# Weights of q and k loaded ahead of the last scratch reads, and projections in the first cycle with scores

## The chip, the cores and the metric

The kernel runs on one core of one Trainium2 chip. A core has TensorE (PE, matmuls), VectorE (DVE), ScalarE (ACT), GpSimd (POOL) and SyncE (SP, which here issues most of the DMAs), a local memory, and eight accumulator banks that TensorE writes and VectorE and ScalarE read. The metric is the device time of one execution in microseconds.

## The reference, cut to what matters

A layer norm of x feeds two branches whose sum is added to x: attention with 32 heads of 16, and a gated MLP whose gate mixes along the sequence.

```python
S, D, H, Dh, Fh = 2048, 512, 32, 16, 896
xn = layernorm(x)
q, k, v = split(xn @ wqkv)                       # per head: S x 16
o = softmax(q @ k.T * Dh ** -0.5) @ v
A = o @ wo
z = gelu(xn @ w_in)
z1, z2 = z[:, :Fh], layernorm(z[:, Fh:])
g = w_sp @ z2 + b_sp[:, None]
out = x + A + (z1 * g) @ w_out
```

## The kernel before, in words

**Number format.** Each dense operand is split into a high and a low part. A dense product is three matmuls (mm3, lines 170 to 172): high by high, low by high, high by low. The split of a weight is a copy (line 196, GpSimd) and a subtraction (line 197, GpSimd).

**Attention.** Heads go in 16 pairs. For each pair there are two passes over the 2048 x 2048 products of q and k. The first finds each row's maximum: `max_mm` (line 650, result "mx") and a reduction on VectorE (line 658, "mm"). The second makes the scores (line 960, "st") from q and k with two more rows that hold the negated maximum, ScalarE takes the exponential (line 58, "pf"), and a matmul with V follows (line 934, "o"). A pair has 64 steps for maxima and 64 for scores. The maxima run LEAD = 27 steps ahead of the scores. When the 16 maxima of a quarter are there, they go through a small scratch (`mscr`) back into rows of q by four SP transfers.

**Where q and k come from.** The projections of q and k come in four blocks of 128 columns, m = 0 to 3, each for four quarters g of the sequence. The block m = 0 is made in the start, before the loop. The blocks 1 to 3 are made by the generator `qk_rest` inside the loop: `qk_group(m, g, ...)` makes a group of 12 matmuls for q (a = 0) and one for k (a = 1). ScalarE copies a group's bank ("qr"), copies its high part ("qkhl"), GpSimd subtracts (line 325), and SP stores the pair to scratch (`qscr`, `kscr`). There are three such buffers. `load_stacks(p)` reads a pair's rows from the scratch into one of two stacks, `qst` and `kst`, with eight transfers; in the start it does so for each quarter.

**The start.** x is loaded, normed, transposed (line 276) and split. Then come, for g = 0 to 3, the groups of m = 0, `load_stacks(0)` for that quarter, and four tiles of V (`v_tile`). The weights of m = 1 are begun (a load) at g = 2 and ended (the split) at g = 3. The weights of m = 2 and 3 are left to `qk_prepare()`, which is put on the list `bg` after the start. `bg` is moved on by one turn per half-step: a turn may start one load (three buffers "raw"), and may split a load that is two half-steps old.

**The loop.** It goes by half-steps, `now[0]` from -18. An even half-step has one maximum and two scores, an odd one two maxima and one score; two half-steps make a cycle of three steps. The 18 half-steps below 0 are called the lead in this document: they have maxima but no scores. In a half-step the dense work is taken from `queue` as long as a credit lasts. In the lead the credit is 2600 per half-step, that is four mm3 of 650, one group. From half-step 0 on, dense work goes only into odd half-steps, at a credit that spreads the work left over the steps left. A generator that lacks its weights returns a pause, and the half-step stays without dense work. All orders are written out in Python when the program is made. On the chip each engine, and each DMA queue, runs its own list in order and waits for semaphores.

**Banks.** Six of the eight banks are three double tiles that maxima and scores take in turn. The last two are called "d" (dense results) and "o" (the product with V). In the start the tiles of V take "d" and "o" in turn. In the lead a group takes "d" for q and "o" for k until half-step -3, and "d" from then on, since "o" belongs to the product with V from the first score cycle on.

Of the kernel before, what the change touches and what calls it, by code (L numbers as in the profile page):

```python
# [23 lines left out]
NG = S // 512  # L24
# [16 lines left out]
def fused_block(ctx, tc, x, wqkv, wo, w_in, w_spT, b_sp, w_out, out):  # L41
# [65 lines left out]
    now = [-2 * LEAD // 3 - 1]  # L107
# [3 lines left out]
    pool = [-1000.0]  # L111
# [41 lines left out]
    def dpsum(nm, tag="d", n=1):  # L153
        left[0] = n
        return ps.tile([P, 512], F32, tag=tag, name=nm, bufs=1)
# [13 lines left out]
    def mm3(acc, lh, ll, rh, rl, first, last):  # L169
        nc.tensor.matmul(acc, lh, rh, start=first, stop=False)  # L170
        nc.tensor.matmul(acc, ll, rh, start=False, stop=False)  # L171
        nc.tensor.matmul(acc, lh, rl, start=False, stop=last)  # L172
# [53 lines left out]
    bg = []  # L226
# [73 lines left out]

    def qk_group(m, g, w, tags=("d",)):
        for a in range(2):
            if now[0] < -2 and m:
                tags = ("d", "o")
            acc = dpsum(f"qk{m}_{a}_{g}", tags[a % len(tags)], ND)
            for c in range(ND):
                t = xnT[g, c]
                mm3(acc, w[a][:, 0, c * P:(c + 1) * P], w[a][:, 1, c * P:(c + 1) * P], t[:, 0, :], t[:, 1, :], c == 0, c == ND - 1)
                yield 650 + 0.5 * (c == ND - 1)
            if m == 0:  # L310
                run(qk_split(m, g, a, acc))
                yield 0
                continue
            raw_ = t512(f"qr{m}_{a}_{g}")
            act(raw_, acc, AF.Copy, 512)
            side.append(qk_split(m, g, a, raw_))
            yield 0

    def qk_split(m, g, a, src):
        hl = hilo(f"qkhl{m}_{a}_{g}")  # L320

        act(hl[:, a, :], src, AF.Copy, 512)
        yield
        if m:
            gps(1.3).tensor_sub(hl[:, 1 - a, :], src, hl[:, a, :].bitcast(F32))  # L325
            yield from pool_done()
        else:
            dve(512).tensor_sub(hl[:, 1 - a, :], src, hl[:, a, :].bitcast(F32))
        (store if m else move)((qscr, kscr)[a][m][:, :, g * 512:(g + 1) * 512], hl)
        yield  # L330

    def qk_prepare():
        yield from prepare(wq, [((m, a), *qk_weights(m, a)) for m in (2, 3) for a in range(2)])
# [15 lines left out]
    def v_tile(t, ws, mid=None):  # L349
        acc = dpsum(f"v{t}", "do"[t % 2])  # L350
        sl = slice((t % 4) * P, (t % 4 + 1) * P)
        for c in range(ND):
            if c == 2 and mid:
                mid(t + 1)
            xt = xnT[t // 4, c]
            mm3(acc, xt[:, 0, sl], xt[:, 1, sl], ws[c][:, 0, :], ws[c][:, 1, :], c == 0, c == ND - 1)
        act(vhead[:, t, :, :DH], acc.rearrange("p (h d) -> p h d", d=DH), AF.Copy, 512)
# [257 lines left out]
    def load_stacks(p, cols=slice(0, S)):  # L615
        m, r = p // 4, (p % 4) * 2
        q, k = qst[p % 2], kst[p % 2]
        sl = [slice((r + j) * DH, (r + j + 1) * DH) for j in range(2)]
        for j in range(2):
            for i, (t, scr) in enumerate(((q, qscr), (k, kscr))):  # L620
                two = t[64 * j:64 * j + 2 * DH, cols], scr[m][sl[j], :, cols]
                one = t[64 * j + 2 * DH:64 * j + KS, cols], scr[m][sl[j], i, cols]
                for args in (two, one):
                    if p and 2 * j + i:
                        later(2 * j + i, move, *args)
                    else:
                        move(*args)
# [200 lines left out]
    def run(gen):  # L828
        for _ in gen:
            pass  # L830
# [9 lines left out]
    with tc.manual_schedule(engines=engines):  # L840
# [46 lines left out]
        for g in range(NG):  # L887
            once = True
            for y in qk_group(0, g, w0, ("d", "o")):
                if y == 0 and once and g < 2:  # L890
                    once = False
                    if g == 0:
                        turn_x(1)
                        norm = norm_x(2)
                    else:
                        next(norm)
            load_stacks(0, slice(g * 512, (g + 1) * 512))
            if g == NG - 2:
                for a in range(2):
                    wq[1, a] = begin(*qk_weights(1, a))  # L900
            if g == NG - 1:
                for a in range(2):
                    wq[1, a] = end(wq[1, a])
            for t in range(4 * g, 4 * g + 4) if g else ():
                next(norm, 0)
                if t % 4 == 2:
                    if g + 1 < NG:
                        turn_x(g + 1)
                    if g + 2 < NG:
                        norm = norm_x(g + 2)  # L910
                v_tile(t, wv)
        steady.append(True)
        bg.append(qk_prepare())
        queue.extend([qk_rest(), z2_all(), z1_all(), spatial(), mlp_out(), attn_out()])
        todo = 650 * (3 * 32 + 112 + 112 + 28 * 16 + 112)
        pause = 0
# [78 lines left out]
        for half in range(-2 * LEAD // 3, 2 * (N // 3 + 4)):  # L995
            b = 3 * (half // 2)
            ms = [b + LEAD] if half % 2 == 0 else [b + LEAD + 1, b + LEAD + 2]
            ns = [n for n in ([b, b + 1] if half % 2 == 0 else [b + 2]) if 0 <= n < N]
            if b + LEAD >= NSTEP:
                ns = [n for n in range(b, b + 3) if n < N] if half % 2 == 0 else []  # L1000
            now[0] = half
            flush()
            for n in ns:
                if n == 16:
                    init_rows(1)
                if n % 64 == 14 and n // 64 + 1 < NP:
                    load_stacks(n // 64 + 1)
            pause = max(0, pause - 1.5)
            final = []
            if NSTEP - LEAD <= b < N and half % 2 and turn and turn[0][0] + 1 in added:  # L1010
                final.append(last_mm(*turn.pop(0)))
            tiles = [(scores, n) for n in ns]
            for i, m in enumerate(ms):
                tiles.insert(1 if half % 2 == 0 else 2 * i, (max_mm, m))
            for make, n in tiles:
                make(n)
            while ended:
                chunk_out(*ended.pop(0))
            for n in ns[:1]:
                exp(n)  # L1020
            if half % 2 == 0:
                pv_some(b - 1, ready // 2 * 2)
            for n in ns[1:]:
                exp(n)
            while behind and behind[0][0] <= half:
                nc.scalar.dma_start(*behind.pop(0)[1:])
            for f in final:
                last_add(*f)
            low = min(load.values())
            for e in load:  # L1030
                load[e] = min(load[e] - low, 2.0)
            limit = load["D"] + (2.5 if half % 2 == 0 else 3.0)
            for m in ms:
                max_red(m)

            if half % 2 == 0:
                for m in range(ms[0] - 2, ms[0] + 1):
                    max_fin(m)
            if drain:
                drain = False  # L1040
                cost = next(queue[0], None)
                if cost is None:
                    queue.pop(0)
                else:
                    pause = -cost
            bg[:] = [g for g in bg if next(g, 0) is None]
            side[:] = [g for g in side if load["D"] > limit or next(g, 0) is None]
            ready += len(ns)
            if b < 0:
                credit = 2600  # L1050
            elif half % 2:
                credit = min(credit + 3 * (max(todo / max(DENSE - b, 10), 600 if b > DENSE - 15 else 0) if todo > 0 else max((todo + 64 * 650) / max(N - 6 - b, 8), 450)), 3250)
            else:
                continue
            if urgent and between and not drain and "ones" in sel:
                queue.insert(0, urgent.pop(0))
                pause = 0
            took = 0
            while queue and not pause and not drain and go():
                cost = next(queue[0], None)  # L1060
                if cost is None:
                    queue.pop(0)
                elif cost <= 0:
                    pause = -cost
                else:
                    drain = between = cost % 1 > 0
                    credit -= cost
                    todo -= cost
                    left[0] -= 1
                    took += 1  # L1070
# [39 lines left out]
```

## Time and profile before

| what | value |
|---|---|
| runs, median (lowest to highest) | 1957.61 us (1957.44 to 1958.38), 3 runs |
| the profiled execution | 1957.17 us, span 1955.4 us |
| TensorE busy | 1936.4 us (99%) |
| VectorE busy | 1374.0 us (70%) |
| ScalarE busy | 1231.1 us (63%) |
| GpSimd busy | 725.1 us (37%) |
| first maximum / first score | 83.68 us / 138.22 us |
| HBM read and written | 144 GB/s over the span |

In the rows of the profile, "out<-in" names the tiles without their numbers, "xN" counts instructions, and the two numbers at the front of a timeline row are the start (from the span's start) and the length in microseconds. What stands in brackets at the end of a row is the idle time of the engine before it and what ended it. SPq rows are issues of DMAs, not the transfers. A row of the table of stretches has: stretch, its length, then busy time of PE, of its weight loads, of DVE, ACT and POOL with the number of instructions, the granted clock of TensorE, the share of the DMA engines and GB/s. A row of waits has the waiting instruction, what ended the wait, us in total, how many, and the longest. A matmul's shown length is longer than the time after which the next can start.

### The profile page before, as it was taken

The numbers are of one execution on the slowest core, as the hardware profiler recorded it, in microseconds if no ns is written. First come the engines' busy times: TensorE is split into PE (matmuls) and PEld (weight loads), VectorE is DVE, ScalarE is ACT, GpSimd is POOL, SyncE is SP. The second block draws the span as 40 slices with busy tenths as digits, with TensorE's granted clock in tenths as the row PEclk, the third lists the DMA queues.
The fourth block names the chain that finished last, engine by engine and source line by source line (L and its number), as shares of the span: only waits on it lengthen the run. The fifth ranks groups of instructions, "written<-read, shape, count | busy, mean of one in ns | idle before, by whom it ended". The sixth has DMA issues, their size and how long they took to land.

```text
span 1955.4 us, 32643 instructions
## 1 busy us (share of the span) xinstructions
PE 1936.4 (99%) x12559; PEld 1050.4 (54%) x12559; DVE 1374.0 (70%) x1565; ACT 1231.1 (63%) x1407; POOL 725.1 (37%) x790
## 2 busy tenths in 40 slices
PE   9999999999999999999999999999999999999998
PEld 7765555555555555555555555555555555555543
DVE  5367777777677677777777777777777777777873
ACT  5346678888677666656666666566666655556664
POOL 3334278889776931126122531017112300002100
PEclk9999999999999999999999999999999999999999
DMA  7566344363535545365545745346454645355323
GB/s 275 198 220 182 99 115 124 114 170 114 141 130 157 181 117 139 109 154 167 137 138 166 200 134 132 104 121 205 111 156 143 174 142 136 112 145 162 105 74 113
DMA packets 229218, 284.23 MB, mean 145 GB/s; under 512 B 35192, under 2 KB 134152, under 8 KB 226184
## 3 DMA queue, kind: packets, MB, share of 16 engines
q1 hardware_dynamic: 217256, 272.64, 48.4%
q0 software_dynamic: 2592, 8.46, 1.1%
q10 hardware_dynamic: 9216, 1.05, 0.4%
q8 instruction: 99, 1.62, 0.3%
q14 instruction: 55, 0.45, 0.1%
HBM read 188.51 MB, written 93.58 MB: 144 GB/s over the span
## 4 chain that ended last, share of the span: by engine, by line
PE 93%; DVE 2%; ACT 2%; DMA 1%; issue 1%; SPq 0%; POOL 0%; DVEq 0%; ACTq 0%
PE o L934 23%; PE mx L650 16%; PE st L960 15%; PE sp L170 7%; PE sp L171 5%; PE sp L172 5%; PE qk L170 2%; PE z1p L170 2%; PE mo L170 2%; PE z2p L170 2%; PE qk L171 1%; PE qk L172 1%; PE z1p L172 1%; PE z1p L171 1%; PE mo L171 1%; PE mo L172 1%
## 5 line engine op out<-in xcount | busy, mean ns | idle before, releaser
L658 DVE TENSOR_REDUCE mm<-mx 128x2 f32<-128x1024 f32 x1024 | 1222.1, 1222 | 498.2 <-PE mx L650 493.9
L58 ACT ACTIVATE pf<-st 128x1024 f32<-128x1024 f32 x1024 | 1027.7, 1025 | 622.5 <-PE st L960 587.4
L934 PE MATMUL o<-pf,vall 128*32 128x512 f32 (+1 forms) x5120 | 511.0, 514 | 0.0
L650 PE MATMUL mx<-kst,qst 48*128 48x512 f32 x2048 | 447.5, 435 | 2.7 <-ACT pf L58 1.8
L960 PE MATMUL st<-qst,kst 50*128 50x512 f32 x2048 | 443.8, 431 | 1.3 <-DVE mm L658 1.0
L650 PEld LDWEIGHTS mx<-kst,qst 48*128 48x128 f32 x2048 | 192.2, 185 | 268.3 <-ACT pf L58 169.6
L960 PEld LDWEIGHTS st<-qst,kst 50*128 50x128 f32 x2048 | 193.2, 185 | 158.9 <-issue 85.6
L934 PEld LDWEIGHTS o<-pf,vall 128*32 128x32 f32 x5120 | 131.5, 109 | 233.3 <-issue 211.4
L170 PE MATMUL sp<-wsp,zs 128*128 128x512 f32 x448 | 194.2, 433 | 0.3 <-DVE z1i L566 0.2
L573 POOL TENSOR_TENSOR z1i<-z1i,hhl 128x512 f32<-128x512 f32 x28 | 36.0, 1286 | 413.9 <-DVE z1i L566 411.5
L171 PE MATMUL sp<-wsp,zs 128*128 128x512 f32 x448 | 176.1, 393 | 0.0
L172 PE MATMUL sp<-wsp,zs 128*128 128x512 f32 x448 | 175.8, 392 | 0.0
L170 PEld LDWEIGHTS sp<-wsp,zs 128*128 128x128 f32 x448 | 83.9, 187 | 69.4 <-issue 52.6
L172 PEld LDWEIGHTS sp<-wsp,zs 128*128 128x128 f32 x448 | 84.2, 188 | 19.5
L171 PEld LDWEIGHTS sp<-wsp,zs 128*128 128x128 f32 x448 | 84.4, 188 | 12.1
L196 POOL CAST wo<-wo0r 128x512 fp32r<-128x512 f32 x1 | 0.6, 611 | 190.1 <-DMA wo0r<-in_wo 190.1
L325 POOL TENSOR_TENSOR qkhl<-qr,qkhl 128x512 fp32r<-128x512 f32 x24 | 30.9, 1289 | 71.4 <-ACT qkhl L58 71.4
L170 PE MATMUL z2p<-w,xt 128*128 128x448 f32 x128 | 51.3, 401 | 0.0
L170 PE MATMUL mo<-wout,hp 128*128 128x512 f32 x112 | 48.6, 434 | 0.6 <-DVE xr L610 0.4
L711 POOL TENSOR_TENSOR ob<-ob 128x512 f32<-128x512 f32 (+1 forms) x16 | 20.6, 1289 | 75.6 <-DMA ob<-rscr 67.7
L172 PE MATMUL z2p<-w,xt 128*128 128x448 f32 x128 | 46.9, 366 | 0.0
L171 PE MATMUL z2p<-w,xt 128*128 128x448 f32 x128 | 46.7, 365 | 0.0
(382 smaller groups left out, 1985.2 us busy)
## 6 DMA issues: line engine op xcount, KB each, us to landing
zs<-z2scr SPq DMA_DIRECT2D x112, 512.0 KB
escr<-e SPq DMA_DIRECT2D x60, 256.0 KB
hscr<-hhl SPq DMA_DIRECT2D x28, 512.0 KB
xscr<-xnT POOLq DMA_DIRECT2D x16, 512.0 KB, 4.8
qscr<-qkhl SPq DMA_DIRECT2D x16, 512.0 KB
kscr<-qkhl SPq DMA_DIRECT2D x16, 512.0 KB
xt<-xscr SPq DMA_DIRECT2D x64, 128.0 KB
z2scr<-z2hl SPq DMA_DIRECT2D x32, 256.0 KB
```

The costliest lines, as they stand in the source:

```text
L58: return nc.scalar.activation(out, in_, func, **kw)
L170: nc.tensor.matmul(acc, lh, rh, start=first, stop=False)
L171: nc.tensor.matmul(acc, ll, rh, start=False, stop=False)
L172: nc.tensor.matmul(acc, lh, rl, start=False, stop=last)
L196: gps(0.6).tensor_copy(t[:, 0, :n], rw[:, :n])
L325: gps(1.3).tensor_sub(hl[:, 1 - a, :], src, hl[:, a, :].bitcast(F32))
L573: gps(1.3).tensor_add(z1, z1, hl[:, 1, :].bitcast(F32))
L650: nc.tensor.matmul(acc[:, j, :], qst[p % 2][rows, tt * P:(tt + 1) * P], kst[p % 2][rows, kc * 512:(kc + 1) * 512], start=True, stop=True)
L658: dve(1024).tensor_reduce(mmax[i // 16][:, :, t, kc], mstep.pop(i), AX.X, ALU.max)
L711: gps(1.3).tensor_mul(both[rows, 0, :], both[rows, 0, :], both[rows, 2, :])
L934: nc.tensor.matmul(acc[cols:cols + VW, a:a + w], vpack(kt - 1 + r, 2 * p + j), pf[:, j * 512 + a:j * 512 + a + w], start=(kt == 1 and a == ...
L960: nc.tensor.matmul(st[:, j, :], kst[p % 2][rows, kt * P:(kt + 1) * P], qst[p % 2][rows, c * 512:(c + 1) * 512], start=True, stop=True)
```

## The change

Four things, all about the projections for m = 1 to 3.

1. At g = 3 of the start, before the last quarter's scratch reads, three turns of `qk_prepare()` are taken with the clock of half-steps set back by two. They issue three loads: both weights of m = 2 and that of q for m = 3.
2. After the start and before the loop, three more turns are taken: they split these three on GpSimd. The fourth weight is loaded in the loop.
3. In half-step 0 and 1, as long as no product with V has been made, the credit is 2600 per half-step, as in the lead.
4. Up to half-step 0 a group's bank goes by the parity of the half-step: "o" in even ones, "d" in odd ones. So half-step 0 takes "o", the bank that V's tiles shared in the start.

```diff
     def qk_group(m, g, w, tags=("d",)):
         for a in range(2):
-            if now[0] < -2 and m:
-                tags = ("d", "o")
+            if now[0] <= 0 and m:
+                tags = ("do"[now[0] % 2 == 0],)
             acc = dpsum(f"qk{m}_{a}_{g}", tags[a % len(tags)], ND)
...
+            if g == NG - 1:
+                now[0] -= 2
+                more = qk_prepare()
+                for _ in range(3):
+                    next(more)
+                now[0] += 2
             load_stacks(0, slice(g * 512, (g + 1) * 512))
...
+        pool[0] = -1000.0
+        for _ in range(3):
+            next(more)
         steady.append(True)
-        bg.append(qk_prepare())
+        bg.append(more)
...
+            fresh = done == 0
...
-            if b < 0:
+            if b < 0 or b == 0 and fresh and not done:
                 credit = 2600
```

## The prediction

> **What bounds the kernel now.** I read the page first, then the table of stretches, then TensorE's waits, then the timeline from 74 to 147 us, where the change lies. From the page:
>
> ```profile
> span 1955.4 us, 32643 instructions
> PE 1936.4 (99%) x12559; PEld 1050.4 (54%) x12559; DVE 1374.0 (70%) x1565; ACT 1231.1 (63%) x1407; POOL 725.1 (37%) x790
> PEclk9999999999999999999999999999999999999999
> PE 93%; DVE 2%; ACT 2%; DMA 1%; issue 1%; SPq 0%; POOL 0%; DVEq 0%; ACTq 0%
> ```
>
> TensorE (PE) is busy for 99% of the span, at its full granted clock, and holds 93% of the chain that ends last; VectorE has 70%, ScalarE 63%. So what can be gained is PE's idle time, and the stretches say where that is (length, then PE busy):
>
> ```profile
> 0.00:83.70 83.70, 80.37 (x369) 65.64 (x369) 34.96 (x81) 36.81 (x67) 24.84 (x42) 1.00 0.69 246
> 83.70:138.20 54.50, 53.62 (x235) 36.98 (x234) 32.72 (x32) 18.76 (x30) 25.44 (x22) 1.00 0.64 222
> 138.20:142.90 4.70, 4.03 (x21) 2.14 (x20) 3.58 (x3) 3.97 (x5) 0.90 (x1) 1.00 0.30 112
> 142.90:1800.00 1657.10, 1654.36 (x10931) 875.22 (x10930) 1204.96 (x1338) 1080.84 (x1207) 660.31 (x711) 1.00 0.51 142
> 1800.00:1955.40 155.40, 144.02 (x1014) 70.46 (x1010) 97.79 (x112) 90.77 (x98) 13.62 (x15) 0.98 0.32 99
> ```
>
> PE idles 3.33 us in the start, 0.88 in the lead (18 half-steps in which maxima run ahead of any score), 0.67 in the first cycle with scores, 2.74 in the 1657 us after it, 11.38 at the end. The change touches the second and third stretch: 1.55 us of idle time. TensorE's waits name it:
>
> ```profile
> PE mx L650 <- ACT pf L58: 1.8, 7, 0.7
> PE st L960 <- DVE mm L658: 1.0, 4, 0.4
> PE mx L650 <- DVE mm L658: 0.9, 1, 0.9
> ```
>
> The 0.9 is one wait of a maxima matmul for VectorE, and the longest of the 1.8 is the 0.67.
>
> **The change part by part.** The listing of the order in which the changed program's matmuls stand has the same matmuls, 9951 as written, and from score 927 on the same order. What differs is where the projections stand. Before, 15 groups of 12 projection matmuls stand in the lead, in 15 of 18 half-steps, because the weights of q and k for m=2 and 3 are not split in time (mx3 to mx6 follow each other bare, and so do mx9 to mx11). After, all 18 half-steps have a group, and the first score cycle has 24 projection matmuls instead of 6. So 36+18 = 54 of them leave later cycles. Rows for it:
>
> ```profile
> 83.68 0.50 PE L650 MATMUL mx<-kst,qst 48*128 48x512 f32 x2
> 90.66 0.97 PE L650 MATMUL mx<-kst,qst 48*128 48x512 f32 x6
> 92.51 0.49 PE L650 MATMUL mx<-kst,qst 48*128 48x512 f32 x2 [0.88 <-DVE mm L658]
> 105.23 0.39 PE L170 MATMUL qk<-xnT,wqk 128*128 128x512 f32 x1
> 105.91 0.39 PE L170 MATMUL qk<-xnT,wqk 128*128 128x512 f32 x1
> 110.30 0.50 PE L650 MATMUL mx<-kst,qst 48*128 48x512 f32 x2
> 110.73 0.50 PE L170 MATMUL qk<-xnT__1034,wqk 128*128 128x512 f32 x1
> 113.68 0.73 PE L650 MATMUL mx<-kst,qst 48*128 48x512 f32 x4
> 117.28 0.50 PE L650 MATMUL mx<-kst,qst 48*128 48x512 f32 x2
> 138.22 0.50 PE L960 MATMUL st<-qst,kst 50*128 50x512 f32 x2
> 142.85 0.50 PE L960 MATMUL st<-qst,kst 50*128 50x512 f32 x2
> 143.76 1.07 PE L934 MATMUL o<-pf,vall 128*32 128x512 f32 x8
> 144.76 0.50 PE L650 MATMUL mx<-kst,qst 48*128 48x512 f32 x2
> 145.81 0.50 PE L170 MATMUL qk<-xnT__1216,wqk 128*128 128x512 f32 x1
> ```
>
> - Price of one projection matmul: L170 to the next L170 is three of them, 105.91-105.23 = 0.68 us, so 0.227 each. Taken out of later cycles: 54 x 0.227 = -12.26.
> - The lead. A half-step with one maximum and 12 projections takes 113.68-110.30 = 3.38, with two maxima 117.28-113.68 = 3.60. Nine of each are 62.82. Before, the lead took 138.22-83.68 = 54.54. So +8.28, for 36 matmuls that are worth 8.17: the 0.88 us wait goes, but three bare half-steps become three dense ones, and every turn from maxima to projections and back costs PE about 0.1 (110.30 to 110.73 is 0.43). Net +0.1.
> - The first score cycle. Before 142.85-138.22 = 4.63. After: score, maximum, score as from 142.85 to 143.76 (0.91), 12 projections as from 110.73 to 113.68 (2.95), maximum, score, maximum as from 144.76 to 145.81 (1.05), 12 projections (2.95): 7.86. That is +3.23 for 18 matmuls worth 4.09: -0.86. The 0.67 us wait for the exponentials is now covered by projections.
>
> Sum so far: 8.28+3.23-12.26 = -0.75. Two costs come from the banks:
>
> ```profile
> 83.78 0.60 ACT L58 ACTIVATE vall<-v 128x512 f32<-128x512 f32 x1 [2.12 <-PE v L172]
> 84.11 0.50 PE L170 MATMUL qk<-xnT,wqk 128*128 128x512 f32 x1
> 143.40 1.94 ACT L58 ACTIVATE pf<-st 128x1024 f32<-128x1024 f32 x2 [0.56 <-PE st L960]
> ```
>
> - The bank now goes by the parity of the half-step. The first (-18, even) takes "o", which the last V tile has just filled; ScalarE empties it until 84.38, while PE came to its first projection at 84.11. Before it took "d". Cost 84.38-84.11, about +0.3.
> - In the second score cycle a new group needs "d", which ScalarE empties after two exponentials: they end 143.40+1.94-142.85 = 2.49 into the cycle, and the copy takes another 0.60 (the row of 83.78 has the same form): 3.09, against PE's arrival at 145.81-142.85 = 2.96. Between 0 and +0.3; I take 0.15.
>
> The loads ahead of the scratch reads, on SP's queue and GpSimd's:
>
> ```profile
> 81.78 0.30 SPq L102 DMA_DIRECT2D kst<-kscr  x1
> 82.19 0.40 SPq L102 DMA_DIRECT2D wqk_0r<-in_wqkv  x1
> 85.39 0.61 POOL L196 CAST wqk<-wqk_0r 128x512 fp32r<-128x512 f32 x1 [15.52 <-DMA wqk_0r<-in_wqkv]
> 86.08 1.29 POOL L197 TENSOR_TENSOR wqk<-wqk_0r,wqk 128x512 fp32r<-128x512 f32 x1
> ```
>
> - Three issues of some 0.5 us pass the eight scratch reads of the last quarter, so these come up to 1.6 us later, plus at most the 85.39-82.19 = 3.2 that a weight load takes, if they queue behind it. Their last was issued by 82.08; with another 3.2 for its own landing that is 82.08+1.6+3.2+3.2 = 90.1. The first matmul that reads that quarter is the fourth maximum, after one half-step of each kind and the 0.3: 83.68+0.3+6.98 = 91.0. Taken as 0; ends 0 and +1.
> - Three splits of 0.61+1.29 = 1.9 stand on GpSimd ahead of everything else in the lead. Even if the loads come no earlier than before, they end at 87.4, 89.3 and 91.2; their groups start at 91.4, 95.0 and 98.4. Cost 0, covered by PE's own work. The fourth weight has 4 more groups of time.
>
> Result: -0.75+0.3+0.15 = **-0.3 us** (-1.2 to +1). The profiled execution took 1957.17 us, 1.8 beyond its span; that gives 1956.9. It lies 0.4 under the median of the runs, 1957.61, so for the median I say **1957.3**. This kernel's measurement can tell about 0.2%, 3.9 us, from no change: I expect no change.
>
> **The rivals.** *Slower: stores pile up behind the read of the first row maxima.* SP waits for it in order, and stores queue behind it.
>
> ```profile
> 114.44 2.79 SPq L102 DMA_DIRECT2D qst<-mscr  x4
> 121.83 0.53 SPq L102 DMA_DIRECT2D kscr<-qkhl  x1
> 129.85 0.63 ACT L58 ACTIVATE qkhl<-qr 128x512 fp32r<-128x512 f32 x1 [4.89 <-DMA kscr<-qkhl]
> ```
>
> Before, ScalarE once stood 4.89 us, for a store issued at 121.83 that freed its buffer at 129.85, 8.0 us later, and PE just got by. After, the sixteenth maximum starts at 83.98+5x6.98 = 118.9; SP is released 114.44-110.30 = 4.1 later and issues the first store behind at 118.9+4.1+2.9 = 125.9, with one projection group more waiting per half-step. ScalarE then needs 0.63+0.60 to empty "o", and PE wants it for group 14 at 83.98+7x6.98+0.43 = 133.3. So a store may take 133.3-125.9-1.2 = 6.2 us; beyond that each us is one of PE. For it: the 8.0 above, which would cost 1.8 a time. Against: that store stood behind four reads of the transposed input, and in the new order none stand there. It takes two such waits and more to be 0.2% slower: +2 to +6, about 1961.
>
> *The scratch reads do come late*, at the fourth maximum: the ends above, +1, and one us for each beyond; 1958 to 1960. [...]
>
> *Later collisions.* All dense work moves forward by some 20 scores, and other transfers meet. In the new order the stack of head pair 4 (eight reads, before from 504.74 on) stands among the fetches of the third quarter of the gate product.
>
> ```profile
> 545.53 0.44 SPq L102 DMA_DIRECT2D xnT__5881<-xscr  x1
> 561.35 0.40 PE L170 MATMUL z1p<-xnT__5881,w 128*128 128x512 f32 x1
> ```
>
> Such a fetch has 15.8 us before its use, so the collision must cost over 10 us to be seen. The waits of this stretch, 2.74 us, could double: 1957 to 1960.
>
> *Faster.* Moved matmuls could save more than 0.227 each where the first cycles hide short waits, and the waits of the long stretch could shrink: 0.3 each would be -4 us in all, 1953.6. No row shows it.
>
> *It doesn't do what it says*: the splits come too late. Then PE would wait at the third half-step, since the order is fixed; the bound above says no.
>
> **How the numbers follow.** Forecast 0.60 (1956.4 to 1958.6, none beyond 0.2%); stores 0.14, half of it beyond +3.9; scratch reads 0.05, 0.01 beyond; late weights 0.01; collisions 0.10, 0.05 beyond; faster 0.10, 0.06 beyond -3.9. So faster 0.06, same 0.81, slower 0.13. The range leaves out the outer tenth on each side: 1955.3 to 1961.
>
> **What would show it.** Right: no pair of bare maxima in the lead; the first projection some 0.3 after 84.1; the first score at about 147; PE idle in the first score cycle near 0; the end of the chain unchanged from score 927 on. Wrong: PE idle over 1 us before a projection of groups 12 to 16, behind a ScalarE copy (stores); an idle PE before the fourth maximum (reads); over 5 us idle in the long stretch (collisions).

## The result, and the profile after

The changed kernel takes **1973.52 us** (median of 6 runs, 1968.17 to 1974.60) against 1957.71 us of the kernel before (6 runs, 1957.44 to 1958.83). The ratio is 1.0074, with a 95% interval of 1.0064 to 1.0085: 15.8 us slower, where 1957.3 was forecast and "no change" had 81% of the chance. Its profiled execution took 1973.37 us, with a span of 1971.6, 16.2 longer than before. From its page (the span, busy times, chain):

```profile
span 1971.6 us, 32648 instructions
PE 1945.2 (99%) x12559; PEld 1051.0 (53%) x12559; DVE 1376.5 (70%) x1568; ACT 1233.4 (63%) x1407; POOL 720.8 (37%) x784
PE 83%; DMA 4%; DVE 2%; ACT 1%; POOL 1%; issue 1%; SPq 1%; ACTq 0%; DVEq 0%; POOLq 0%
```

Two things grew. TensorE's idle time went from 19.0 to 26.4 us, and its busy time from 1936.4 to 1945.2 with the same 12559 matmuls: some of them ran slower. The table of stretches shows where (length, busy time of PE, of its weight loads, of DVE, ACT and POOL, granted clock, DMA share, GB/s):

```profile
83.80:147.42 63.62, 63.27 (x274) 43.55 (x272) 33.01 (x32) 22.66 (x36) 26.18 (x22) 1.00 0.68 239
147.42:156.60 9.18, 7.81 (x38) 5.33 (x37) 3.59 (x3) 5.21 (x7) 3.41 (x4) 1.00 0.52 166
156.60:160.62 4.02, 1.98 (x16) 0.65 (x16) 1.23 (x1) 3.06 (x4) 1.08 (x2) 1.00 0.53 188
160.62:167.44 6.82, 6.82 (x26) 3.67 (x26) 3.48 (x3) 2.58 (x3) 6.50 (x9) 0.50 0.12 36
1116.35:1119.76 3.41, 1.72 (x14) 0.75 (x18) 2.08 (x3) 1.02 (x1) 3.25 (x5) 1.00 0.42 93
1119.76:1123.18 3.42, 3.42 (x22) 1.09 (x14) 0.46 (x1) 1.02 (x1) 1.35 (x3) 0.50 0.92 340
1123.18:1815.00 691.82, 690.14 (x4552) 360.02 (x4552) 504.95 (x554) 417.43 (x438) 144.25 (x141) 1.00 0.50 141
```

The lead (first row) is as forecast: 0.35 us idle in 63.62. The first score cycle takes 9.18 instead of the 7.86 forecast. In the next 4.02 us TensorE is idle for half, and then, for 6.82 us, it has a granted clock of 0.50. The same pair, a stall of half a piece of 3.41 us and a piece at half clock behind it, stands once more at 1116 to 1123. TensorE's largest waits from the lead to the end of the dense work:

```profile
PE mx L650 <- ACT pf L58: 2.1, 6, 1.0
PE o L943 <- ACT qr L58: 2.0, 1, 2.0
PE st L969 <- DMA qst<-mscr: 1.7, 1, 1.7
PE qk L170 <- ACT qr L58: 1.4, 1, 1.4
PE st L969 <- DVE mm L658: 0.8, 3, 0.4
PE sp L172 <- POOL wsp L197: 0.6, 1, 0.6
PE mo L170 <- DMA hp<-hscr: 0.4, 1, 0.4
```

Two of these are new in kind: waits for "qr", ScalarE's copy of a projection group's bank. The timeline of PE and ACT around them:

```profile
148.33 0.50 PE L170 MATMUL qk<-xnT__1350,wqk 128*128 128x512 f32 x1
152.09 1.02 ACT L58 ACTIVATE pf<-st 128x1024 f32<-128x1024 f32 x1 [0.97 <-PE st L969]
153.01 0.59 ACT L58 ACTIVATE qr<-qk 128x512 f32<-128x512 f32 x1
153.66 0.50 PE L170 MATMUL qk<-xnT__1350,wqk 128*128 128x512 f32 x1 [1.37 <-ACT qr L58]
157.14 1.94 ACT L58 ACTIVATE pf<-st 128x1024 f32<-128x1024 f32 x2 [2.82 <-PE st L969]
158.96 0.60 ACT L58 ACTIVATE qr<-qk 128x512 f32<-128x512 f32 x1
159.62 1.06 PE L943 MATMUL o<-pf,vall 128*32 128x512 f32 x8 [2.04 <-ACT qr L58]
160.62 0.79 PE L650 MATMUL mx<-kst,qst 48*128 48x512 f32 x2
```

The group that starts at 148.33 is copied out at 153.01, behind an exponential, and only then does the next group start (153.66). That one is copied out at 158.96, behind two exponentials, and only then does the first product with V start (159.62). So both groups and the product share one bank, "o". The code says why, and I had misread it: `tags` is set in half-step 0 to `("o",)`. In half-step 1 the condition `now[0] <= 0` is false, so the line is passed over, and the variable keeps "o" from the turn before. I had taken it that the second group gets "d".

The other new wait, at 1118.62, in the timeline (rows of SP and ACT are issues):

```profile
1105.01 0.33 ACTq L1036 DMA_DIRECT2D mscr<-ms  x1
1115.03 2.70 SPq L102 DMA_DIRECT2D qst<-mscr  x4
1118.62 0.88 PE L969 MATMUL st<-qst,kst 50*128 50x512 f32 x2 [1.69 <-DMA qst<-mscr]
```

and the same two transfers in the kernel before:

```profile
1089.55 0.33 ACTq L1026 DMA_DIRECT2D mscr<-ms  x1
1094.35 2.91 SPq L102 DMA_DIRECT2D qst<-mscr  x4
```

After, the read of the row maxima is issued 10.0 us after their store (1105.01 to 1115.03), before, 4.8. The waits of SP's queue from 1104 to 1119 us, after, name what it stood for instead:

```profile
SPq L102 <- POOL wsp L197: 3.5, 3, 2.1
SPq L102 <- DMA zs<-z2scr: 3.5, 1, 3.5
```

Seven loads of spatial weights now stand among the eight reads of a stack and these maxima (before, two), and SP waits in order for GpSimd to free their buffers and for a fetch to land. This is read from the order of the queue; no run takes these loads away. It is also a matter of the execution: with the same order of SP's transfers and only one bank changed (the first experiment below), the read is issued 8.2 us after its store (1098.3 to 1106.5), and no matmul waits there. The new order makes the place tight, and whether it fails differs.

The 16.2 us, then: waits for "o" 3.41 (1.37 + 2.04), the half clock behind them 6.82 x 0.5 = 3.41, the late maxima 1.69 and their half clock 1.71, the other new waits of the long stretch 2.1 (1.0 for an exponential, 0.63 and 0.45), and 1.1 at the end, where the last 8 matmuls, which before ran at full clock, fall into half clock. The moves that were forecast at -0.3 stand against that. That leaves some 3 us: 0.5 of it is the start (the first maximum at 84.20 instead of 83.68), and where the rest comes from was not found. It is hardly in TensorE's waits: beside those named, the stretch from 167.44 to 1815 idles 3.1 us, and the long stretch of before had 2.74.

### The profile page after: what moved, and what is told of

Read it like the earlier page. It is cut to its first block, busy times and chain, and to the rows that moved or that the text cites. A ratio compares the mean times of both kernels' runs of the same rounds, so it can differ in the third digit from the quotient of the medians.

```text
span 1971.6 us, 32648 instructions
## 1 busy us (share of the span) xinstructions
PE 1945.2 (99%) x12559; PEld 1051.0 (53%) x12559; DVE 1376.5 (70%) x1568; ACT 1233.4 (63%) x1407; POOL 720.8 (37%) x784
## 3 DMA queue, kind: packets, MB, share of 16 engines
q10 hardware_dynamic: 9216, 1.05, 0.4%
## 4 chain that ended last, share of the span: by engine, by line
PE 83%; DMA 4%; DVE 2%; ACT 1%; POOL 1%; issue 1%; SPq 1%; ACTq 0%; DVEq 0%; POOLq 0%
PE o L943 22%; PE st L969 14%; PE mx L650 14%; PE sp L170 7%; PE sp L172 5%; PE sp L171 5%; PE z2p L170 2%; PE mo L170 2%; PE z1p L170 1%; PE z2p L172 1%; PE z2p L171 1%; PE mo L172 1%; PE mo L171 1%; PE z1p L171 1%; PE z1p L172 1%; PE ao L170 1%
```

## The experiments

The lines of those kernels that have an added line at the top are one higher than above.

| kernel | median, us | ratio to before (95%) |
|---|---|---|
| changed kernel | 1973.52 | 1.0074 (1.0064 to 1.0085) |
| second group on "d" | 1966.93 | 1.0053 (1.0036 to 1.0070) |
| parts 1 and 2 alone | 1962.41 | 1.0027 (1.0016 to 1.0038) |
| without part 3 | 1963.21 | 1.0030 (1.0017 to 1.0043) |
| before, with stalls | 2003.08 | one run |
| "d", given back by score 90 | 1968.70 | 1.0059 (1.0044 to 1.0073) |
| before, dense work moved forward | 1967.48 | 1.0053 (1.0040 to 1.0066) |
| before, DENSE 921 | 1974.39 | 1.0085 (1.0071 to 1.0100) |
| "d", DENSE 921 | 1989.41 | 1.0162 (1.0148 to 1.0177) |
| "d", given back by score 300 | 1968.55 | 1.0056 (1.0043 to 1.0069) |
| changed kernel, given back by score 300 | 1971.47 | 1.0074 (1.0061 to 1.0088) |
| parts 1 and 2, later splits | 1962.08 | 1.0027 (1.0016 to 1.0038) |
| "d", given back by 300, no bare cycle | 1958.64 | 1.0008 (0.9999 to 1.0017) |

### Another bank for the second group

```diff
-            if now[0] <= 0 and m:
+            if now[0] <= 1 and m:
```

> One edit on the changed kernel: the second projection group of the first score cycle takes bank d instead of o; the order on every engine stays. Theory 'one bank': the groups of half-steps 0 and 1 and the first product with V all take bank o, because the name chosen in half-step 0 is kept for half-step 1; this makes TensorE wait 1.37 + 2.04 us for ScalarE's copies, and its clock then stands at 0.5 for 6.83 us. Then both waits go, the clock stays at 1.00 there, and the time falls by 1.4 + 2.0 + 3.4 = 6.8 us, less some 0.2 for the next group that needs d: 1966.9. Rival 'late ScalarE': the copies come late behind the exponentials whichever bank is used; then the waits only move to the groups on d, over 1.5 us are left, and the time stays at 1971 to 1974.

Measured: 1966.93 us. No instruction moved on any engine; only the bank of one group is another. The stretches of the lead and of the first score cycle, and then, from the timeline, the group and the copy that had been tied together:

```profile
84.00:147.35 63.35, 63.00 (x273) 43.57 (x272) 33.01 (x32) 22.69 (x36) 26.00 (x22) 1.00 0.67 240
147.35:156.10 8.75, 8.75 (x46) 5.87 (x50) 3.83 (x4) 5.70 (x8) 3.07 (x3) 1.00 0.55 171
```

```profile
152.08 0.50 PE L170 MATMUL qk<-xnT__1350,wqk 128*128 128x512 f32 x1
152.88 0.59 ACT L58 ACTIVATE qr<-qk 128x512 f32<-128x512 f32 x1
```

TensorE is busy for all of the 8.75 us; the second group starts at 152.08, before the copy of the first (152.88). The first cycle took 155.07 - 147.28 = 7.79, for which 7.86 had been forecast, and the clock stays at 1.00. "Late ScalarE" falls: the copies are as late as before, and nobody waits. From the first score to score 9 the changed kernel takes 23.50 us and this one 17.22, so 6.3 us are saved there, where the 1.37 + 2.04 + 3.41 of above less 0.2 were expected. The medians differ by 6.6, but the runs of each kernel spread by some 6 us, so that this comes so close to the sum is luck; the two profiled executions differ by 9.8, since the late maxima don't fail in this one.

What is left, between the medians, is 9.6 us over the kernel before.

### The parts apart

Parts 1 and 2 alone:

```diff
-            if now[0] <= 0 and m:
-                tags = ("do"[now[0] % 2 == 0],)
+            if now[0] < -2 and m:
+                tags = ("d", "o")
...
-            if b < 0 or b == 0 and fresh and not done:
+            if b < 0:
```

> Parts 1 and 2 alone (loads and splits ahead); the first score cycle and the bank rule are as before. Theory 'one bank plus phase': no wait for o in the first cycles, so the 6.8 us are gone, but the dense work still stands 42 matmuls earlier at every score, so transfers of the long stretch still meet in other ways than before; I expect 1958 to 1967, above the 1957.7 of before. Rival 'the banks are all of it': what is lost later is only a consequence of the first stall; then 1957.4 +- 0.5.

Without part 3 only (the second half of that diff):

> The changed kernel without part 3 only (no dense work at full credit in the first score cycle); the bank by parity stays up to half-step 0. Theory 'one bank': the group that met a full bank o is no longer there, so no wait over 0.5 us in the first two score cycles and no stretch at half clock there; start as in the run with parts 1 and 2 alone, within 0.5 us, and the same time within 2 us. Rival 'the bank rule itself costs, in the lead too': over 1 us idle between 83 and 147 us.

Measured: 1962.41 and 1963.21 us, the same within their spread. The lead of the second idles 0.25 us in 62.60, so the bank rule costs the forecast 0.3 there and no more. The start is as good as forecast, and still 5 us are lost, in the long stretch: that is "phase". Part 3, once its bank is mended, adds 3.7 to 4.5 between the medians (1966.93 less these), but the intervals overlap, so this is not clear of the noise. In the profile of parts 1 and 2 alone the largest wait goes back through three engines (a row of PE's timeline, then the waits of ACT from 665 to 676 us and of POOL from 640 to 671):

```profile
672.35 0.80 PE L650 MATMUL mx<-kst,qst 48*128 48x512 f32 x2 [2.12 <-ACT pf L58]
```

```profile
ACT z L58 <- POOL z L364: 3.1, 1, 3.1
POOL wsp L196 <- DMA wsp_6r<-in_w_spT: 1.9, 1, 1.9
```

A maxima matmul waits 2.12 us for an exponential. On ScalarE that exponential stands behind a step of the GELU, which waits 3.1 us for GpSimd; and on GpSimd that step stands behind the split of a weight, for whose load GpSimd had stood idle for 1.9 us. TensorE's clock is 0.50 in the 3.41 us behind it.

### What a stall costs

```diff
+STALL = {96 + 96 * k: 4 + 3 * k for k in range(9)}
...
             for n in ns[:1]:
+                if n in STALL:
+                    for _ in range(STALL[n]):
+                        nc.scalar.activation(ident, ident, AF.Copy)
                 exp(n)
```

> The kernel before with 4, 7, 10, ... 28 idle copies of 128 columns put ahead of the exponential at scores 96, 192, ... 864, so that TensorE stalls by rising amounts. Theory 'a stall is paid twice': the granted clock goes to 0.5 for one or two pieces of 3.41 us once the idle time within some 3.4 us is over about 1.5 us, as after the waits of 1.69 (3.41 us at 0.5) and 2.04 (6.83 us at 0.5) in the changed kernel, and not after stalls of 1.0 and less; a stall of 2 us then costs 2 + 1.7 to 3.4. Rival 'the low clock has another cause' (a load on the chip, heat): no stretch at 0.5 follows the longer stalls, or they come without one.

The stalls that came of it, the four shortest in PE's timeline, and the stretches around two of them:

```profile
488.43 0.50 PE L651 MATMUL mx<-kst,qst 48*128 48x512 f32 x2 [1.70 <-ACT pf L59]
661.88 0.51 PE L651 MATMUL mx<-kst,qst 48*128 48x512 f32 x2 [0.76 <-ACT pf L59]
834.58 0.50 PE L651 MATMUL mx<-kst,qst 48*128 48x512 f32 x2 [1.80 <-ACT pf L59]
1007.21 0.50 PE L651 MATMUL mx<-kst,qst 48*128 48x512 f32 x2 [2.67 <-ACT pf L59]
```

```profile
485.68:489.09 3.41, 1.71 (x16) 0.43 (x8) 0.36 (x2) 3.25 (x8) 3.33 (x4) 1.00 0.73 177
489.09:495.92 6.83, 6.64 (x18) 4.53 (x18) 2.31 (x2) 3.01 (x6) 5.99 (x7) 0.50 1.03 338
830.42:833.83 3.41, 2.36 (x22) 0.59 (x18) 1.23 (x1) 3.12 (x11) 0.00 (x0) 1.00 0.00 0
833.83:837.24 3.41, 2.49 (x12) 1.53 (x12) 2.12 (x2) 3.01 (x4) 0.00 (x0) 1.00 0.13 51
837.24:840.66 3.42, 3.42 (x23) 1.36 (x22) 2.61 (x4) 2.42 (x3) 0.47 (x1) 1.00 0.60 186
```

The stall of 1.70 us is followed by 6.83 us at half clock; the one of 1.80, longer, by none, as the last two rows show. They lie differently on a grid. The half-clock stretches of one execution whose rows are shown here begin whole multiples of 3.413 us apart and last one or two of these pieces (in the changed kernel 281 pieces lie between 160.62 and 1119.76, in the kernel before with its dense work moved, below, 277 between 426.71 and 1372.20). The 1.70 lies wholly in the piece that ends at 489.09; 101 pieces later, at 833.83, the 1.80 is cut into 1.05 and 0.75. Eight pieces of five kernels (before, changed, this one, "parts 1 and 2 alone", "dense work moved forward") had 1.69 to 2.67 us idle at full clock, and half clock followed each. It also followed four pieces with less: 1.16 in the changed kernel, 1.17, 1.19 and 1.24 in that with "d" given back by score 300. It did not follow 0.92 and 1.05 in this one, 1.14 and 1.37 in the changed kernel, and 1.50 in the kernel before (from 1932.88 on). The four longer stalls (3.85, 4.20, 5.57, 5.90) each have their 6.8 or 10.2 us at half clock. The eight stalls come to 26.5 us; behind them the matmuls spent 37.9 us at half clock. Half of that, 18.9, is lost by estimate: in the changed kernel two projection matmuls start 0.43 us apart at 0.50 (162.78 and 163.21), and 0.23 at 1.00. Together 45.4. The execution was slower by 2003.08 - 1957.36 = 45.7, but it was 1.6 us late already at its first score, after a piece at half clock in the start (11.22 to 14.64) that no stall of these explains; from the first score to the last it lost 44.1, which is 1.3 less than the sum. So "a stall is paid twice" holds in this run for six of the eight stalls, 1.70 us and 2.67 to 5.90, and not for the 0.76 nor for the 1.80 that is cut in two: 2.8 to 3.3 us come on top of each of the six, and in other runs 1.7, where a single piece follows. Where half clock lasted for four pieces (13.65 us, once, in the kernel with "d" and DENSE 921), TensorE was busy for 12.5 of them, and it cost 6.2.

### Is it the phase?

Four runs change nothing but how the dense work stands against the scores. The first is made from the changed kernel with the bank mended. GOAL is the list of the dense work left after each half-step in another of the kernels, here before's. What this kernel is ahead of it shrinks to nothing at score 90 (one more line, which sets the credit where the list ends, is not shown):

```diff
+GOAL = {3: 530392.0, 5: 527791.5, 7: 526491.5, ...}
...
-            while queue and not pause and not drain and go():
+            goal = GOAL.get(half, 0) - 1300 * round(max(0, 11700 * (1 - b / 90)) / 1300) + 10
+            while queue and not pause and not drain and (todo > goal if half in GOAL else go()):
```

> The changed kernel with the bank mended, and the 54 early matmuls given back: from half-step 3 to score 90 the dense work is thinned until it stands where it stood before; from there on every engine and queue has the order of the kernel before. Theory 'phase': what was lost after the first cycles (1966.9 - 1957.4 = 9.5 us, of which 8.3 + 3.2 + 0.8 - 12.3 = 0 is the work moved) comes only from how the dense work, its loads and its GpSimd steps now meet the scores; with the old order from score 90 on this goes, and the time is 1957.0 (1956.2 to 1958.2), same as before. Rival 'the start': the loads and splits ahead leave a lasting cost; then 1963 to 1967.

The kernel before, with the mirrored edit (the list of the changed kernel with the bank mended, "+ 1300" for "- 1300"):

> The kernel before, with its own start, loads, banks and first score cycle, whose dense work is thickened up to score 90 until it stands where that of the changed kernel with the bank mended stands; from there on the order of that kernel. None of the change's four parts is in it. Theory 'phase': the late waits of that kernel come back (ScalarE behind GpSimd near scores 280 and 552, the last fetches near score 927), some 3 to 9 us in all: 1960 to 1966. Rival 'the start': 1957.4 +- 1, same as before.

The kernel before with `DENSE = 921` for 931, and the changed kernel with the bank mended and the same:

> The kernel before with the dense work spread so that it ends ten scores earlier (DENSE 921 for 931): the same work, another phase against the scores, nothing of the change. Theory 'phase': any such shift meets waits that the order before does not have; 1959 to 1967, and TensorE's idle time between 143 and 1790 us over 5 us (2.7 before). Rival: only this change's shift costs; 1957.4 +- 1.5.

> The changed kernel with the bank mended and the same shift, DENSE 921. Theory 'phase': other waits than at 931, at other places, the time anywhere from 1957 to 1968 and not tied to the 1966.9 of 931. Rival 'the start': 1966 to 1968 again.

Measured: 1968.70, 1967.48, 1974.39 and 1989.41 us. The first missed its number, by 11.7 us, and taught most. Score by score against the kernel before, it is 12.5 us late at score 96 and stays between 12.2 and 13.1 to score 1008: with the old order nothing is lost any more, so "phase" holds from there on. All of its loss lies ahead of score 96: some 1.5 us in the start, where this execution too had a piece at half clock (11.28 to 14.69), and the rest where the work was given back (below).

The second settles it: the kernel before with none of the four parts, only its dense work moved, is 10.3 us slower. Its stretches, and its largest waits:

```profile
423.30:426.71 3.41, 1.28 (x12) 0.30 (x4) 0.20 (x1) 3.38 (x5) 2.75 (x10) 1.00 0.01 2
426.71:433.54 6.83, 6.71 (x18) 4.39 (x18) 2.43 (x2) 1.68 (x3) 6.75 (x7) 0.50 0.74 203
1368.79:1372.20 3.41, 1.28 (x4) 0.53 (x4) 1.83 (x2) 0.80 (x1) 2.46 (x4) 1.00 0.53 197
1372.20:1379.03 6.83, 6.68 (x23) 2.58 (x23) 2.35 (x3) 2.57 (x4) 2.52 (x2) 0.50 0.37 119
```

```profile
PE mx L651 <- ACT pf L59: 3.4, 5, 2.1
PE sp L171 <- POOL wsp L197: 1.6, 1, 1.6
PE mo L171 <- DMA hp<-hscr: 1.2, 1, 1.2
```

Two stalls (an exponential, a split on GpSimd) with 6.83 us of half clock each. They stand near scores 155 and 690, not at 280 and 552, as I had said, and I did not find what makes one of many tight places the one that fails in a given execution. The last two say the same more strongly: the order before is a good one among its neighbours. All three of these runs lie above the range that was expected of them. Ten scores earlier cost it 17 us (one wait of 4.1 us for `hp<-hscr`, and at the end of the dense work scores that wait for maxima), and cost the mended kernel 22 (three stalls of 3.8 to 4.1 us).

### What giving work back costs

The first run above gave 54 matmuls back in 30 cycles. Counted over the cycles (three scores each) from score 9 to 899, in all the kernels alike, a cycle with 12 dense matmuls takes 6.18 us, with 9 5.50, with 6 4.82, which is 0.227 each; with 3 it takes 4.2, and with none 4.16 (medians). Below some 3 the cycle is VectorE's, not TensorE's: in that run TensorE's scores wait 6.4 us, in 14 waits, for VectorE's maxima. So a matmul taken from a thin cycle gains nothing, and idle time comes instead. A slower return, by score 300:

```diff
-            goal = GOAL.get(half, 0) - 1300 * round(max(0, 11700 * (1 - b / 90)) / 1300) + 10
+            goal = GOAL.get(half, 0) - 1300 * round(max(0, 11700 * (1 - b / 300)) / 1300) + 10
```

> As the run in which the early matmuls were given back by score 90, but given back slowly, up to score 300, so that the cycles are thinned by some 0.5 matmul each and stay long enough for VectorE. Theory 'phase': the 12.4 us of the fast return came from thin cycles in which TensorE waits for VectorE's maxima; with the slow return these go, the old order holds from score 300 on without loss, and what is left are chance waits between 6 and 300: 1956.5 to 1960, most likely 1957.5. Rival 'the start costs': 1963 or more, with the offset to the kernel before already over 4 us at score 48.

and the same edit on the changed kernel as it is, "o" and all:

> The changed kernel as it is (its second group still on the full bank o), with the same slow return up to score 300. If the two causes add, this is the run with the bank mended plus the 1.4 + 2.0 + 3.4 = 6.8 us less some 0.2 of the first cycles: 1964 if that one takes 1957.5. If the late waits are only a consequence of the first stall, this one shows them again and stands above 1968.

Measured: 1968.55 and 1971.47 us. Both missed their numbers. The rival's sign, over 4 us late at score 48, was badly chosen: the first is 10.8 us late there, but the 48 matmuls that it has done by then beyond before's are 10.9, so the start costs nothing. The return did not become free, though. Its largest wait, and two of its stretches:

```profile
PE st L970 <- DVE mm L659: 7.5, 15, 0.9
```

```profile
599.45:602.86 3.41, 2.17 (x22) 0.91 (x22) 3.41 (x3) 2.57 (x3) 2.00 (x3) 1.00 0.84 269
602.86:606.27 3.41, 3.41 (x19) 1.01 (x11) 0.89 (x2) 1.36 (x2) 0.47 (x1) 0.50 0.58 169
```

My rule took away work in pieces of 6, and where a cycle had only 6 it left none: 5 cycles are bare, 3 have three. In a bare one TensorE waits 0.86 and 0.3 to 0.4 us for VectorE's maxima, and behind three of them the clock went to 0.50. The traces of the pair also show that the bank's cost adds to the rest: the two stand 0.3 us apart at the first score, 5.1 at score 12 and still 4.8 at the last, where the stalls are 1.37 + 2.04 and the 3.41 us that stood at half clock this time cost 1.71. The medians differ by 2.9, and their intervals overlap.

So the last one keeps two matmul triples in every cycle where the queue has them (two cycles still have one):

```diff
-            while queue and not pause and not drain and (todo > goal if half in GOAL else go()):
+            while queue and not pause and not drain and (todo > goal or took < 2 if half in GOAL else go()):
```

> As the slow return by score 300 with the bank mended, but every cycle keeps at least 6 dense matmuls where the queue has them, so that none is left bare; the run of the slow return had 5 bare cycles and 3 with three matmuls, and three stretches of 3.41 us at half clock behind them. Theory 'bare cycles': a cycle of 3 scores takes 4.82 us with 6 matmuls and 4.16 with 3 or with none, so 5 bare ones lose some 3.4 us, their half clock 3 x 1.7 = 5.1, together 8.5 of its 10.2 us; without them 1959 to 1961, and the order of before from score 300 on adds nothing. Rival 'the start': 1966 or more again. A kernel faster than before is not expected of it, since the most that the mended change can save here is below 1 us.

Measured: **1958.64 us**, ratio 1.0008 (0.9999 to 1.0017), the same as before. Its two stretches, up to where the old order holds and behind it:

```profile
146.90:660.00 513.10, 510.69 (x3400) 271.79 (x3398) 381.10 (x435) 394.01 (x479) 367.68 (x426) 1.00 0.48 131
660.00:1800.00 1140.00, 1138.44 (x7510) 596.82 (x7508) 826.28 (x904) 689.43 (x728) 292.20 (x285) 1.00 0.52 145
```

It has the changed start, the dense first cycle and the moved weights, no stretch at half clock, and 2.4 and 1.6 us idle. "The start costs" falls. What the change has to give is less than its measurement can tell. None of the kernels is faster than the one before.

### One collision taken away

On parts 1 and 2 alone:

```diff
-                flight.append((now[0] + 2, k, begin(*a)))
+                flight.append((now[0] + (4 if out is wsp and k[0] == 0 else 2), k, begin(*a)))
```

> Parts 1 and 2 alone, with the splits of the first 16 blocks of the spatial weights two half-steps later than before, so that GpSimd doesn't stand idle for a weight that has not landed (1.94 us at 654 us in the run of parts 1 and 2 alone, ahead of the gelu step for which ScalarE, and behind it an exponential and TensorE, waited 2.1 us). Theory 'late load, GpSimd, ScalarE, TensorE': the wait of 2.1 us near 672 us and the 3.41 us at half clock behind it go, 1962.4 - 3.8 = 1958.6, if the shift of these splits meets nothing else. Rival 'GpSimd simply has too much to do there': the wait stays over 1.5 us, 1962 or more.

Measured: 1962.08 us, not different from the 1962.41 of parts 1 and 2 alone. The wait of 2.1 us and its half clock are gone, as the first theory said, but the time isn't: with the weights split later the dense queue runs dry, and from score 294 to 318 seven cycles have three matmuls instead of six or more. The chain is shown; that it can be mended there for a gain is not.

## Why the prediction was wrong

**Right.** The lead: 147.42 - 84.20 = 63.22 us for 62.82 + 0.35. The wait for "o" ahead of the first group: 0.35 for 0.3 (the last V tile's copy ran from 84.31 to 84.91, and the group started at 85.05; the profile names GpSimd, whose splits it doesn't need). The scratch reads and the splits: the fourth maximum started at 91.58 without a wait, and the splits ended by 88.2. The stores behind the first row maxima: ScalarE waited 2.5 us for one, and TensorE for none, so that rival didn't happen. The first score cycle without its bank: 7.79 for 7.86. The order from score 927 on, and the 0.227 per matmul. The sum of the start: from the first maximum to the second score cycle the kernel before takes 59.18 us, and with 8.28 + 3.23 + 0.3 on top that is 70.99; the five kernels with "d" take 70.99 to 71.02. So the forecast of the place that it looked at was right, but for the bank.

**The step that failed first** is "In the second score cycle a new group needs 'd'", a cost of 0 to 0.3. It was a reading of the code, and wrong: the group of half-step 1 keeps "o", and so has to wait for the copy of the group before it, and V's product for its own. I had priced a bank that the code doesn't take. The same working could have been done for "o": the copy stands behind an exponential and ends 6.2 us into the cycle (153.01 + 0.59 - 147.42), and TensorE is there at 4.9. 3.41 us of waits, 3.41 of clock; the run with "d" is 6.3 faster in this place.

**The term that was missing** is the clock. The sum priced a wait at its length. In the trace of before no wait from the lead to the end of the dense work is over 0.9 us, and the clock is at 1.00 as long as there are matmuls; nothing in it shows that a longer wait costs 1.7 to 3.3 us more. But I moved work into a place where I could not rule out such a wait, and gave it no price of this kind. The run with stalls shows it: 18.9 us of clock on top of 26.5 us of stalls, for 44.1 measured.

**The rival that was mis-sized** is "Later collisions", with 1957 to 1960 and a chance of 0.10. I argued that a fetch has 15.8 us before its use, and so has to be very late. But I looked at one transfer. What failed were others: the read of the row maxima, GpSimd's steps ahead of ScalarE's, the fetches of `hp`. With the bank mended these are 9.6 us, and 10.3 in the kernel before when only its work is moved. "The waits of this stretch, 2.74 us, could double" was no bound: in the kernel before that stretch is nearly free of waits only because of where its work happens to stand.

**What stays open.** Which of the tight places fails is not the same from one order to the next, and the times of the kernels here that are slower than before spread by 3 to 7.5 us over their runs, where those of the kernel before spread by 0.8 to 2.5. Which change in the loads would make the long stretch robust wasn't found.

## What to carry to other kernels

When a bank or a buffer is chosen by a variable that outlives its branch, write down for each group of the changed stretch which one it takes, who emptied it last and what stands ahead of that copy; the order of instructions alone doesn't show it. Where TensorE is the bound, look in the trace at the granted clock behind a stall, and price that too: here 1.7 to 3.3 us came on top of most stalls of 1.69 us and more, while one of 1.80, cut in two by the grid, cost nothing beyond itself. And where a kernel's background work is laid out by hand against its loop, moving that work is a change to every later meeting of queues: it is not free because the sum of the work is the same (here it cost 10.3 us in the kernel before), and a thinned cycle gives back only what lies above the next engine's bound (here VectorE's, 4.16 us a cycle).

## What the runs showed that I had not expected

The granted clock changed on a grid of 3.413 us in these executions, and a stall's place on it made a difference: 1.80 us cut in two cost no more than themselves, 1.70 in one piece cost 3.3 more. Half-clock stretches came in 1, 2, 3 and once 4 pieces (3.41, 6.83, 10.24, 13.65 us), and stalls of nearly the same length got one or two. And a shift of ten scores in 931 of the kernel before, with the same instructions' work, made it 0.85% slower, as much as the change under study.
